# A gated linear attention and a dense gated MLP on one core: priorities of a scheduler replaced by a written order of 2439 operations

## The chip, the core and the metric

The kernel runs on one core of one Trainium2 chip. The core has five engines that each work through their own queue in order: TensorE (PE in the profile, its weight loads PEld), VectorE (DVE), ScalarE (ACT), GpSimd (POOL) and SyncE (SP), which here issues every DMA. The metric is the device time of one execution in microseconds. Three runs of the kernel before took 643.52, 644.41 and 644.46 us; the median is 644.41.

## The reference

The input has 4 batches, 8 heads, 768 time steps and 48 features per head. For each head a 48 x 48 state is carried through time. Every row of the state is multiplied by a complex decay whose size is clipped below 0.999, and the outer product of key and value is added:

```python
mag = np.sqrt(a_re * a_re + a_im * a_im)
scale = np.minimum(mag, 0.999) / (mag + 1e-06)
new_re = ar * S_re - ai * S_im
new_im = ar * S_im + ai * S_re
S_re, S_im = (new_re + k v^T, new_im)
y_t = q_t @ S_re
```

The outputs of all heads side by side are 3072 tokens of 384 features. They pass through `h = x @ w_in` (384 x 2048), `g = h * tanh(softplus(h))` and `g @ w_out` (2048 x 384). The two weight matrices arrive as 64-bit floats; everything else is float32.

## The kernel before

**Tiling.** The work is cut into 12 units (`UNITS`): three stretches of 256 time steps for each batch. A unit has two chunks, a and b, of 128 steps (`C`). A unit goes through three parts.

*Elementwise part* (`ew_steps`). From the decay come its size and its angle. Both are summed over time by scans on VectorE (lines 333 and 347). ScalarE supplies the logarithms, exponentials, arctangent and sines. The queries are multiplied by the running decay and the keys by its inverse (`grow`, line 375), and both are turned by the running angle (`rot`, line 397). The exponential and logarithm belong to one activation table, the sine and arctangent to another, so ScalarE loads a table (line 131, ACT_TABLE_LOAD) each time it passes from one to the other. The turned queries and keys are then laid out anew by DMAs from tile to tile (`relay`, line 388). Units 0 and 1 do this part chunk by chunk, the others for both chunks at once.

*Attention* (`attn_steps`). For each chunk TensorE transposes the keys (line 462), forms the 128 x 128 products of keys and queries (line 470), forms the output from them and from the old state (line 486), and the new state (line 502). VectorE masks the products (line 473) and adds the states (line 508); GpSimd fades the state (line 510), except in unit 0. The output is laid out anew by four DMAs (line 521) and split into a high part `xH` and a rest `xL` (lines 157 and 158).

*Gated MLP* (`moe_steps`). The 2048 hidden features are cut into 8 pairs of 128. For each pair `mm1` multiplies on TensorE in three terms, wH·xH, wH·xL and wL·xH (line 548, 18 matmuls), into a PSUM tile `ph`, of which there are three. ScalarE and VectorE form the gate: exp, a cap (line 553), square, ln, exp on ScalarE, a product with `ph` (line 558), then the split of the result into `gh` (line 157) and `gl` (line 158). `mm2` multiplies by the second weights, again in three terms (line 576, 12 matmuls), and adds into PSUM over the pairs. The program places `mm2` of a pair 3.5 pairs behind its `mm1`.

**Weights.** Each matrix is brought in as 12 pieces of 512 columns. The first matrix has room for all of it (`raw_in`, two halves); the second has a tile `wraw` with two buffers. `convert` turns the 64-bit pattern into a float32: ScalarE rounds the low words, VectorE shifts and joins the high ones (lines 190, 194), GpSimd adds the rounded bits (line 199), then the high part is copied on ScalarE or VectorE (line 157) and the rest subtracted on VectorE (line 158), all in one step.

**Units 0 and 1 have a halved MLP.** Their pairs are interleaved in runs of four (`slots`). With `cut`, the partial sums of the first four pairs are stored in DRAM (line 585), read back (line 588) and added (line 589), so that the second half of the weights is needed later.

**Order.** Every step gets a place on a common scale by tuned constants (`EW`, `AT`, `WP`, `LD` and others), and from it a priority. The scheduler of the language, with its own timeline model, picks the order of every engine's queue. `after` adds ordering edges, among them those that keep ScalarE's table loads together. Thirty matmuls of no use (`spin`, line 434) run on TensorE ahead of the attention and ahead of the MLP of unit 0.

## Time and profile before

| | |
|---|---|
| Three runs, median (lowest, highest) | 644.41 us (643.52, 644.46) |
| Profiled execution, span from first to last instruction | 645.8 us |
| TensorE busy (4480 matmuls) | 583.5 us, 90% |
| VectorE busy (877 instructions) | 500.8 us, 78% |
| ScalarE busy (785) | 490.7 us, 76% |
| GpSimd busy (99) | 119.9 us, 19% |
| ACT_TABLE_LOAD on ScalarE | 45 of 1283 ns |
| DMA | 67.05 MB, mean 104 GB/s |

The span is the profile's own time of the one execution it shows; the runs are timed without it. "Busy" counts the time in which an engine has an instruction at work; where two instructions of an engine overlap, that time is counted once. The granted clock (PEclk) is the share of TensorE's full clock that was granted in a stretch; matmuls take longer where it is low.

### The profile page before, as it was taken

The page shows a single profiled execution, that of the slowest core. Times are in us where ns is not written, and L with a number is a line of the kernel's source. Part 1 is how long each engine was busy: PE and PEld are TensorE (multiplying, and loading weights), DVE is VectorE, ACT ScalarE, POOL GpSimd, SP SyncE. Part 2 cuts the span into 40 slices and gives each one's busy share as a digit, 9 for nine tenths or more (in the row PEclk, how much of TensorE's full clock was granted, in tenths as well). Part 3 has the DMA queues.
Part 4 walks back from the last instruction along what each step waited for, and adds up shares of the span by engine and source line. Part 5 has one row for each costly group of instructions (what it writes and reads, how often), then busy time and mean ns, then how long its engine had stood idle before and what let it go on. Part 6 is the DMA issues. An engine that isn't in the chain of part 4 may idle for free.

```text
span 645.8 us, 11762 instructions
## 1 busy us (share of the span) xinstructions
PE 583.5 (90%) x4480; PEld 554.0 (86%) x4480; DVE 500.8 (78%) x877; ACT 490.7 (76%) x785; POOL 119.9 (19%) x99
## 2 busy tenths in 40 slices
PE   0698975888699989999999999999999999999996
PEld 0386854877699989999999999999999999999995
DVE  6989899899769869859868867977788796644551
ACT  6966977677686987977988977888898878655561
POOL 2323446326203003003003003003021030000000
PEclk9956988798899999999999999999999999999999
DMA  8859533612930450450540620711712503101000
GB/s 301 264 184 247 162 115 106 176 38 75 239 103 25 119 154 1 130 141 13 134 125 25 173 75 26 197 50 53 192 28 70 152 5 101 46 25 26 1 26 29
DMA packets 58528, 67.05 MB, mean 104 GB/s; under 512 B 4960, under 2 KB 51040, under 8 KB 58464
## 3 DMA queue, kind: packets, MB, share of 16 engines
q1 hardware_dynamic: 58464, 66.23, 35.9%
q8 instruction: 37, 0.61, 0.4%
q14 instruction: 27, 0.22, 0.1%
HBM read 36.96 MB, written 5.51 MB: 66 GB/s over the span
## 4 chain that ended last, share of the span: by engine, by line
PE 68%; DVE 12%; DMA 7%; issue 4%; POOL 3%; ACT 3%; SPq 2%; POOLq 0%; DVEq 0%
PE po L576 26%; PE ph L548 24%; PE pa L470 6%; PE ypsum L486 6%; PE pd L502 3%; DMA T<-QK 2%; PE pkn L462 2%; DVE wx L190 1%; DMA raw<-w_in 1%; POOL raw L199 1%; DMA R<-a_re 1%; DMA wraw<-w_out 1%; ACT e L123 1%; DVE e L553 1%; SPq L388 1%
## 5 line engine op out<-in xcount | busy, mean ns | idle before, releaser
L576 PE MATMUL po<-wo,gh 128*128 128x384 f32 x768 | 220.8, 348 | 11.3 <-DVE wo L157 7.4
L548 PE MATMUL ph<-xH,wiH 128*128 128x256 f32 x576 | 167.7, 293 | 6.2 <-DVE g L558 5.6
L548 PE MATMUL ph<-xL,wiH 128*128 128x256 f32 x576 | 166.9, 290 | 5.2 <-DVE xL L158 5.2
L548 PE MATMUL ph<-xH,wiL 128*128 128x256 f32 x576 | 166.6, 289 | 0.0
L123 ACT ACTIVATE e<-e 128x512 f32<-128x512 f32 x192 | 119.9, 630 | 52.8 <-DVE e L553 51.1
L576 PEld LDWEIGHTS po<-wo,gh 128*128 128x128 f32 x768 | 142.0, 190 | 16.9 <-DVE wo L157 7.7
L576 PE MATMUL po<-wo,gl 128*128 128x384 f32 x384 | 131.6, 343 | 0.0
L548 PEld LDWEIGHTS ph<-xH,wiH 128*128 128x128 f32 x576 | 112.3, 196 | 9.4 <-DVE g L558 6.0
L548 PEld LDWEIGHTS ph<-xL,wiH 128*128 128x128 f32 x576 | 113.0, 196 | 6.4 <-DVE xL L158 6.4
L548 PEld LDWEIGHTS ph<-xH,wiL 128*128 128x128 f32 x576 | 112.7, 196 | 0.0
L558 DVE SCALAR_TENSOR_TENSOR g<-e,ph 128x512 f32<-128x512 f32 x96 | 65.4, 681 | 25.5 <-ACT e L123 24.9
L553 DVE TENSOR_SCALAR e<-e 128x512 f32<-128x512 f32 x96 | 58.1, 605 | 32.9 <-ACT e L123 32.7
L123 ACT ACTIVATE e<-ph 128x512 f32<-128x512 f32 x96 | 56.8, 593 | 28.7 <-PE ph L548 28.2
L576 PEld LDWEIGHTS po<-wo,gl 128*128 128x128 f32 x384 | 73.1, 190 | 0.4 <-issue 0.4
L510 POOL TENSOR_TENSOR S<-S,T 96x384 f32<-96x384 f32 x18 | 23.0, 1279 | 266.4 <-DVE S L508 113.9
L158 DVE TENSOR_TENSOR gl<-g,gh 128x512 fp32r<-128x512 f32 x96 | 70.8, 737 | 1.6
L123 ACT ACTIVATE e<-e,fifth 128x512 f32<-128x512 f32 x96 | 69.2, 721 | 1.8
L157 DVE CAST gh<-g 128x512 fp32r<-128x512 f32 x96 | 41.4, 432 | 35.1 <-PE po L576 33.5
L375 POOL TENSOR_TENSOR QK<-QK,X 128x1536 f32<-128x1536 f32 (+1 forms) x12 | 40.2, 3353 | 103.2 <-ACT X L123 90.7
L131 ACT ACT_TABLE_LOAD x45 | 57.7, 1283 | 1.6 <-PEq L773 0.8
L470 PE MATMUL pa<-T 96*128 96x128 f32 x384 | 52.0, 287 | 0.0
L470 PEld LDWEIGHTS pa<-T 96*128 96x128 f32 x384 | 48.9, 201 | 0.9 <-issue 0.7
(88 smaller groups left out, 826.2 us busy)
## 6 DMA issues: line engine op xcount, KB each, us to landing
T<-X SPq DMA_DIRECT2D x72, 129.0 KB, 2.5
T<-QK SPq DMA_DIRECT2D x72, 129.0 KB, 3.8
raw<-w_in SPq DMA_DIRECT2D x12, 512.0 KB, 8.3
wraw<-w_out SPq DMA_DIRECT2D x12, 512.0 KB, 3.7
QK<-q SPq DMA_DIRECT2D x12, 384.0 KB, 3.9
QK<-k SPq DMA_DIRECT2D x12, 384.0 KB, 5.0
V<-v SPq DMA_DIRECT2D x12, 384.0 KB, 4.3
out_dram<-o SPq DMA_DIRECT2D x24, 192.0 KB, 1.9
```

Of the source, the lines that this page charges most:

```text
L123: ins = nc.scalar.activation(out, in_, func, **kw)
L131: ins = nc.scalar.preload_act_table_set(name)
L157: heng(h, src)
L158: leng(out=lo, in0=src, in1=h.bitcast(F32), op=ALU.subtract)
L375: (nc.vector if g in FAST and u == 0 else nc.gpsimd).tensor_tensor(QK[..., :C], QK[..., :C], X[..., :C], ALU.mult)
L470: nc.tensor.matmul(pa[:, i, :], st["T"][c][:, 4 * g + i, 1, :C], st["T"][c][:, 4 * g + i, 0, :C], start=True, stop=True)
L486: nc.tensor.matmul(py[64 * par:64 * par + D, i, :], lhs, rhs, start=n == 0, stop=first or n == 1)
L510: (nc.vector if u < WIDE else nc.gpsimd).tensor_tensor(nS, nS, pe, ALU.mult)
L548: nc.tensor.matmul(ph[:, a, :], wi[wp][:, j, kt, a * P:a * P + P], st[xp][:, kt, :], start=n == 0, stop=n == 8)
L553: nc.vector.tensor_scalar_min(e, e, math.exp(20.0))
L558: nc.vector.scalar_tensor_tensor(g, e, 2.5, ph, ALU.subtract, ALU.mult)
L576: nc.tensor.matmul(po[t], gp[:, a, tsl], wo[part][:, wp, 2 * i + a, :], start=j in starts and a == 0 and n == 0, stop=j + 1 in ends and a ...
```

## The change

All steps are recorded in a list (`Work`): for each operation its engines, a name and a function. There are 2439 of them. `ORDER` gives the sequence in which they are issued, under the language's manual schedule, so each engine's queue follows this sequence; a letter behind a number moves the operation to another of its engines. The table loads of ScalarE come wherever the written sequence passes from one table's functions to the other's.

The weights come as 16 pieces of 768 columns, one of each matrix for each pair of hidden features. A piece is loaded into one of two buffers `words` and joined into a float32 tile `w` (`weight`). Its split into high part and rest is recorded apart (`halves`); the rest is written into the tile of the piece before it.

The halved MLP with its stores and loads in DRAM is gone: all units run pairs 0 to 7. The two turns of a tile by the angle (line 397 before) are one instruction with a broadcast operand. `gl` has two buffers in place of three. Six groups of four spin matmuls stand in the order between the attention of chunk a of unit 1 and the first `mm1`. `good`, a count by which a general path is chosen when inputs are out of bounds, is kept.

```diff
-ADDV = 12
-HACT, HMOD = 2, 3
...
+WC = DM * DF // P // NPAIR
+NW = 2 * NPAIR
+SPLIT_UNITS = 2
+PLAIN = 0
+SPINS, SPIN = 6, 4
...
+ORDER = [(int(x.rstrip("VAGTS")), x.lstrip("0123456789")) for x in """
+0 1 3 6 2 4 7 127 10 340 8 560 339 30 11 5 9 13 16 343 12 27 559 132 14 17 28 19 18 31 29 20 36 32 15 21 34 33 35 24
...
+2408 2419A 2427 2398 2428 2429 2409 2420 2430 2410 2431A 2421 2432 2422 2433 2434 2435 2437 2436 2438
+""".split()]
...
+    def act(self, out, in_, func, **kw):
+        need = TABLE.get(func)
+        if need and need != self.table:
+            self.nc.scalar.preload_act_table_set(need)
+            self.table = need
+        return self.nc.scalar.activation(out, in_, func, **kw)
+
+    def issue(self, tc):
+        order = ORDER or [(i, "") for i in range(len(self.ops))]
...
+        for i, other in order:
+            engines, name, f = self.ops[i]
+            e = other or engines[0]
...
+            f(self.engines[e])
...
+    def weight(i):
...
+        def load(e):
+            words[i] = me.tile([P, WC], I64, tag="words", name="words", bufs=2)
+            e.dma_start(words[i], src)
...
+        op("S", f"w{i} load", load)
+        op("A", f"w{i} low", low)
+        op("V", f"w{i} shift", shift)
+        op("V", f"w{i} join", join)
+        op("GV", f"w{i} carry", carry)
+
+    def halves(i):
...
+        op("AV", f"w{i} high", high)
+        op("V", f"w{i} rest", rest)
...
+            op("VG", f"{n} grow", grow)
+            op("VGA", f"{n} ends q", ends("QK"))
+            op("VGA", f"{n} ends x", ends("X"))
...
+            op("V", f"{n} turn sin", turn("X", "X1"))
...
+                op("VG", f"{n} S fade", fade)
...
+                gs[j].append(me.tile([P, 2, TU], F32R, tag="gl", name="gl", bufs=2))
...
+                op("VA", f"{n} gh", high(j))
...
-    for u in range(NUN):
-        slot = slots.get(u, range(NPAIR * u, NPAIR * (u + 1)))
...
-        moe = moe_steps(units[u], u * TU, u, u < 2)
...
+    with tc.manual_schedule():
+        op.issue(tc)
...
-    with tile.TileContext(nc, schedule_with_timeline_sim=True) as tc:
+    with tile.TileContext(nc) as tc:
```

More of the change, by code (lines that the diff above doesn't have):

```diff
@@ L1 @@
 import math
-from contextlib import ExitStack
 import numpy as np
@@ L150, in tile_kernel @@
[L150 to L158 removed]
+    good = const.tile([P, UNITS + SPLIT_UNITS, 3], F32, name="good")
+    ncar = const.tile([P, NJ], F32, name="ncar")
@@ L424, in ew_steps, with load, f @@
[L424 to L437 removed]
+        def load(n, src, g):
+            def f(e):
+                x = src[u].rearrange("p (a t) -> p a t", t=C)
+                e.dma_start(flat(st[n], g), x[:, g * NJ:g * NJ + NJ] if isinstance(g, int) else x)
+            return f
@@ new lines, in load_qk, with f, load_v @@
+        def load_qk(a, src):
+            def f(e):
+                e.dma_start(both(st["QK"], slice(0, NCH))[:, :, a, :C], src[u].rearrange("p (a t) -> p a t", t=C))
+            return f
+        def load_v(e):
+            st["V"] = io.tile([P, NCH, DM], F32, tag="V", name="V", bufs=2)
+            e.dma_start(st["V"], v[u])
+        agroups = groups if u == 0 else (slice(0, NCH),)
+        for g in agroups:
+            op("S", f"R{u} load {gi(g) if u == 0 else u}", load("R", are, g))
+            op("S", f"I{u} load {gi(g) if u == 0 else u}", load("I", aim, g))
@@ L494, in yv @@
-                return f
-            def upd():
-                nS = at.tile([2 * D, H, D], F32, tag="S", name="S", bufs=2)
-                for g in range(2):
-                    pd = bank([2 * D, 4, D], "pd", "pd", c)
+                                lhs = st["V"][:, c, h * D:(h + 1) * D] if new else old["S"][:, h, :]
+                                rhs = d["am", h // 4][:, h % 4, :] if new else T()[:, h, 0, :C]
+                                e.matmul(ypsum[64 * par:64 * par + D, i, :], lhs, rhs,
+                                         start=m == 0, stop=first or m == 1)
@@ new lines, in f, with fade @@
+                        e.tensor_tensor(d["S"][:, sl, :], d["pd", g], old["S"][:, sl, :], ALU.add)
+                return f
+            def fade(e):
+                pe = T()[:, :, 0, C].unsqueeze(2).broadcast_to([2 * D, H, D])
+                e.tensor_tensor(d["S"], d["S"], pe, ALU.mult)
+            if not last:
+                for g in range(2):
+                    op("T", f"{n} kn{g}", kn(g))
+                    op("AV", f"{n} kn out{g}", kn_out(g))
+            for g in range(2):
+                op("T", f"{n} am{g}", am(g))
+                op("V", f"{n} am out{g}", am_out(g))
@@ new lines, in chunk, with move, f @@
+            for g in range(2):
+                op("T", f"{n} y{g}", y(g))
+            op("AV", f"{n} y out", y_out)
+            if not last:
+                for g in range(2):
+                    op("T", f"{n} pd{g}", pd(g))
+                    op("V", f"{n} S add{g}", add(g))
+                op("VG", f"{n} S fade", fade)
+        for c in range(NCH):
+            chunk(c)
+        def move(p0, j, r0, n):
+            def f(e):
+                e.dma_start(st["x"][p0:p0 + 4 * n, j, :], st["y"][r0:r0 + n].rearrange("r i t -> r (i t)"))
+            return f
@@ new lines, in attention, with high, f, rest @@
+        for r, run in enumerate(XRUNS):
+            op("S", f"u{u} x move{r}", move(*run))
+        if u < PLAIN:
+            return
+        def high(j):
+            def f(e):
+                (e.copy if e is nc.scalar else e.tensor_copy)(st["xH"][:, j], st["x"][:, j])
+            return f
+        def rest(j):
+            def f(e):
+                e.tensor_tensor(st["xL"][:, j], st["x"][:, j], st["xH"][:, j].bitcast(F32), ALU.subtract)
+            return f
+        for j in range(NJ):
+            op("AV", f"u{u} xH{j}", high(j))
+            op("V", f"u{u} xL{j}", rest(j))
```

892 lines of the change are left out of this document (415 added, 477 removed), and 16 rows, old and new, of the table ORDER.

## Prediction

> **What bounds the kernel now.** I read the page first, for the shares of the engines; then busy time in windows, to find where TensorE is not full; then the chain of waits, for the price of TensorE's work; then the groups of instructions of two stages.
>
> ```profile
> span 645.8 us, 11762 instructions
> PE 583.5 (90%) x4480; PEld 554.0 (86%) x4480; DVE 500.8 (78%) x877; ACT 490.7 (76%) x785; POOL 119.9 (19%) x99
> ```
>
> ```profile
> 0.00:16.00 16.00, 0.00 (x0) 0.00 (x0) 10.77 (x28) 11.01 (x20) 4.35 (x18) 1.00 0.86 301
> 16.00:160.00 144.00, 113.15 (x744) 97.89 (x746) 135.23 (x233) 109.84 (x184) 61.52 (x40) 0.81 0.51 152
> 160.00:240.00 80.00, 72.41 (x560) 70.29 (x556) 62.25 (x113) 61.39 (x99) 9.96 (x7) 0.96 0.49 133
> 240.00:384.00 144.00, 143.11 (x1170) 137.58 (x1167) 115.55 (x197) 120.66 (x188) 18.37 (x14) 1.00 0.33 92
> 384.00:416.00 32.00, 32.00 (x263) 31.68 (x262) 28.34 (x47) 26.89 (x44) 6.43 (x5) 1.00 0.32 89
> 416.00:639.60 223.60, 222.88 (x1757) 216.58 (x1756) 148.67 (x266) 160.40 (x255) 19.30 (x15) 1.00 0.22 59
> 639.60:646.00 6.40, 0.00 (x0) 0.00 (x0) 0.00 (x0) 0.49 (x1) 0.00 (x0) 0.82 0.21 69
> ```
>
> The columns are the stretch, its length, the busy time of PE, PEld, DVE, ACT and POOL, the granted clock, and DMA. There are three stages. **Stage 1**, to 160 us: VectorE is busy 10.77 + 135.23 = 146.0 us, from 16 us on 94% of the time, while TensorE waits and runs at a clock of 0.81. **Stage 2**, 160 to 384 us: TensorE is almost full; VectorE has 62.25 + 115.55 = 177.8 us of 224 and ScalarE 61.39 + 120.66 = 182.05. **Stage 3**, to 639.6 us: TensorE is full. The last matmul ends there, and 6.2 us of output follow.
>
> TensorE's work at full clock has these prices:
>
> ```profile
> 173.48 1.51 PE pkn L462 x8
> ...
> 259.21 2.12 PE po L576 x12
> 261.33 2.12 PE ph L548 x18
> 263.45 1.90 PE ypsum L486 x32
> ...
> 269.79 1.32 PE pd L502 x16
> ...
> 284.77 1.78 PE pa L470 x16
> ...
> 635.48 4.10 PE po L576 x22
> ```
>
> Twelve units have 96 pairs at 2.12 + 2.12 us, 20 chunks at 1.51 and at 1.32, 24 at 1.78 and 22 at 1.90 (four chunks have no old state): 407.0 + 56.6 + 84.5 = 548 us. The last matmul ends at 639.6 us, so 91.5 us are lost before it. After 160 us there were 479.6 us, of which 9.2 were idle by the windows and 4% of 72.4 lost to the clock: 467.5 us of work. So 548 − 467.5 = 80.5 us are done by 160, the loss is 79.5 us in stage 1, 11.7 in stage 2 (224 us for 212.3 of work) and under 1 in stage 3.
>
> **The change part by part.** The matmuls are the same. I count the written order off from its end with the prices above. 467.5 us of TensorE's work are left behind the `mm1` of pair 4 of unit 1 (166 half `mm1` and 176 half `mm2` at 1.06 us, and 132 attention groups), and 253 behind the first `mm1` of pair 2 of unit 6. These two places end stages 1 and 2 of the new kernel. Then I count what VectorE, ScalarE and GpSimd have ahead of each.
>
> *VectorE in stage 1, work moved.* I price what differs from the trace, in which 22 of 24 weight pieces and 11 pairs were through by 160 us.
>
> ```profile
> L158 DVE TENSOR_TENSOR wiL<-raw,wiH 128x512 fp32r<-128x512 f32 x12 | 9.6, 800 | 1.7 <-ACT wiH L157 1.7
> ...
> L375 DVE TENSOR_TENSOR QK<-QK,X 128x768 f32<-128x768 f32 x2 | 1.9, 946 | 0.1
> ```
>
> Five of 16 carries move from GpSimd to VectorE. The nearest row is the subtraction, 0.80 us for 512 columns, so 1.2 for 768: +6.0 us (0.64 a carry if it ran at the 0.43 us that a one-operand instruction takes below: +3.2). The `grow` of units 1 and 2 moves too, four such halves at 0.946: +3.8. All weights instead of 22 of 24 are ready, about +4.7; three more fades, small copies, +2. Against that only one high part of 16 is copied on VectorE, before seven of 24, −3; three `gh` go to ScalarE and fewer pairs are begun, −4; the turns, squares and angles of this stretch are fewer, −4.5. The sum is about +5.
>
> *VectorE in stage 1, stalls.* One and the same instruction, the cap at line 553, is long while GpSimd works and short otherwise:
>
> ```profile
> 301.36 2.10 DVE L553 TENSOR_SCALAR e<-e 128x512 f32<-128x512 f32 x1
> ...
> 306.68 0.43 DVE L553 TENSOR_SCALAR e<-e 128x512 f32<-128x512 f32 x1 [0.18 <-ACT e L123]
> ```
>
> ```profile
> 299.58 3.59 POOL L375 TENSOR_TENSOR QK<-QK,X 128x1536 f32<-128x1536 f32 x1 [25.76 <-ACT X L123]
> ```
>
> The long one ends 0.3 us behind the end of GpSimd's `grow`. The groups of stage 1 carry the same excess, the first and second here:
>
> ```profile
> L190 DVE TENSOR_SCALAR wx<-raw 128x512 uint32<-128x512 uint32 x12 | 11.5, 955 | 0.0
> ...
> L355 DVE COPY ncar<-I 128x3 f32<-128x3 f32 x3 | 2.6, 863 | 0.0
> ```
>
> ```profile
> L199 POOL TENSOR_TENSOR raw<-raw 128x512 int32<-128x512 int32 x12 | 19.8, 1659 | 29.2 <-DVE raw L194 28.0 <-ACT wiH L157 1.1
> ```
>
> Line 190 at 0.955 instead of 0.43 is 6.3 us too long, and with the other groups, each against the shortest of its shape, I count 20.8 us. GpSimd was busy 4.35 + 61.52 = 65.9 us in this stage. In the written order it has 11 carries and nothing else up to the stage's end: 11 x 1.659 x 1.5 = 27 us. If the excess falls with GpSimd's time, 12 us of the 20.8 go; bounds 0 and 20.8. So VectorE needs 146.0 + 5 − 12 = **139 us** (130 to 155).
>
> The Trainium skill (SBUF — State Buffer, Who interferes with whom) says that VectorE and GpSimd lock a port for a whole instruction and that whichever comes second waits it out; the two rows agree. By it 11 carries can still hold up VectorE 11 times for up to 2.5 us, 27 us, so that all of the excess could stay: stage 1 would then be 12 us longer than I say below.
>
> *ScalarE.* Counted along the order, it changes its table 17 times in stage 1 (13 in the trace), 30 in stage 2 (18), 61 in all (45).
>
> ```profile
> L131 ACT ACT_TABLE_LOAD x13 | 16.7, 1283 | 1.0 <-PEq L773 0.8
> ```
>
> ```profile
> L131 ACT ACT_TABLE_LOAD x18 | 23.1, 1283 | 0.3
> L123 ACT ACTIVATE X<-X 128x768 f32<-128x768 f32 x15 | 12.7, 848 | 0.0
> ```
>
> ```profile
> L157 ACT CAST wiH<-raw x8: 635/664/690, 27.3 to 127.7; 128x512 fp32r<-128x512 f32 x8
> ```
>
> ```profile
> 309.21 1.28 ACT L131 ACT_TABLE_LOAD   x1
> 310.51 0.85 ACT L143 ACTIVATE X<-I 128x768 f32<-128x768 f32 x1
> ```
>
> Stage 1: 4 loads are 5.1 us, high copies of 15 pieces at 1.0 instead of 15 at 0.66 another 5, and `gh`, small copies and the earlier start of the next units some 5: 120.85 + 15 = 136 us, still below VectorE's. Stage 2: 12 loads are 15.4 us; 75 elementwise operations of 768 columns stand in it for 60, 15 x 0.85 = 12.8; 7 `gh` at 0.66 are 4.6; fewer copies out of PSUM and no weights, −5. That is +28, and since ScalarE's groups of this stage add up to 196.8 us for 182.05 busy (neighbours overlap), +26: **208 us** of ScalarE against 212.3 of TensorE. VectorE, by the same count, comes to some 195. Stage 3 is left with under 190 us for each of them against 253.
>
> The Trainium skill (ScalarE: Activation LUTs, What ACT_TABLE_LOAD costs) adds a drain of about 1.38 us to each switch. The two rows above show the next operation 0.02 us behind the load, so I leave it out; by the page, an estimate, 30 switches would put 41 us more on ScalarE in stage 2.
>
> *How long the stages are then.* The unknown is how full an engine that bounds can be kept. VectorE as the bound of stage 1 was 94% busy (135.23 of 144), with single windows at both ends:
>
> ```profile
> 32.00:48.00 16.00, 15.98 (x105) 14.26 (x103) 13.01 (x28) 9.88 (x19) 4.49 (x6) 0.50 0.56 193
> ...
> 96.00:112.00 16.00, 9.03 (x52) 8.50 (x51) 16.00 (x18) 11.12 (x15) 10.75 (x7) 0.82 0.37 107
> ```
>
> ```profile
> 352.00:416.00 64.00, 63.98 (x531) 61.92 (x530) 52.75 (x90) 55.34 (x86) 7.33 (x6) 1.00 0.39 107
> ```
>
> I take 94% for both bounds. Stage 1: 16 + (139 − 10.8)/0.94 = **152 us**, 8 less. Stage 2: 208/0.94 = **221 us**, 3 less than 224. Stage 3 and the output stay. So the span is 645.8 − 11 = 635; the runs' median is 1.4 below the profiled span, which gives **634 us**.
>
> *Edits that I cost at nothing.* Dropping the halves saves four stores, four loads and four additions on VectorE, which the counts above hold already or are coarser than. The spins are 24 for 30 and run while TensorE has nothing else; none stands ahead of unit 0's attention now, which at clock 0.50 takes twice its 12 us, hidden since TensorE has 79.5 us to lose in stage 1; without that cover, 12 us. Two `gl` buffers make VectorE wait for the `mm2` two pairs back, with the caps and gates behind it; in the order that `mm2` always stands ahead of the `gl`, by at least two operations, and such a wait can only grow where TensorE is late, that is, full. The tail of the order ends with ten half `mm2`, as the trace ends with a run of such matmuls.
>
> **Weights through two buffers.** The first matrix had room for itself; now 16 pieces share two buffers.
>
> ```profile
> raw<-w_in SPq DMA_DIRECT2D x12, 512.0 KB, 8.3
> wraw<-w_out SPq DMA_DIRECT2D x12, 512.0 KB, 3.7
> ```
>
> A piece has 768 KB: 5.6 us by the lower row, 12.5 by the upper, and about 5 until its carry frees the buffer (1.0 + 1.0 + 2.5 and gaps). That is 5.3 to 8.8 us a piece and 85 to 140 us for all. The last piece is wanted by pair 7 of unit 0, where VectorE has 95% of its stage 1 work behind it, at 144 us. I take the lower row, since the upper is from six loads issued at once, and it is hidden.
>
> **The rivals.**
>
> *ScalarE becomes the bound of stage 2 and is served worse (slower).* Its queue is in order; square, ln and exp of a pair wait for VectorE's cap, and all that stands behind waits too. For it: 208 against 212.3 us leaves no slack, and ScalarE was never above 86% (55.34 of 64) over any long window while TensorE was full. Against: nothing asked it for more. At 86.5% stage 2 takes 240 us: +16 − 8, span 654, median **653**. It decides from 208/(224 + 8) = 90% downward.
>
> *Both bounds are kept full (much faster).* All waits of stage 1 behind 16 us go, and stage 2 is TensorE's 212.3: 16 + 128 = 144 and 212, −16 − 12, median **617**. For it: windows of 16.00 us of 16. Against: three engines above 92% at once, which no stage of the trace shows.
>
> *The weights come late (no change).* With 12.5 us a load and some queueing behind relays on SyncE's queue, pair 7 of unit 0 slips by 8 us and the gain of stage 1 is gone; with ScalarE below 94%, 3 us of stage 2 too: **644**.
>
> *The order isn't what decides (the change doesn't do what it says).* If a table switch did cost a second 1.3 us, stage 2 would be 247/0.94 = 263 us and the median 673; the gap of 0.02 us speaks against it.
>
> **How the numbers follow.** Forecast, both bounds near 94%, median 624 to 643: 0.54. Both full: 0.14. ScalarE served worse: 0.21. Late weights: 0.10, over half of it within 0.2%. A costlier switch: 0.01. Faster by over 0.2%, about what a measurement of this kernel can tell from no change, is then 0.54 + 0.14 + 0.02 = 0.70; the same 0.07; slower 0.23. The range for 8 in 10 goes from both full, 617, to ScalarE served worse, 653. The likeliest case's own range is 624 to 643.
>
> **What would show it.**
>
> ```profile
> L553 DVE TENSOR_SCALAR e<-e 128x512 f32<-128x512 f32 x96 | 58.1, 605 | 32.9 <-ACT e L123 32.7
> ```
>
> Right: TensorE's share passes 95% before 155 us, VectorE busy over 94% ahead of that, ScalarE at 90% or more from then to about 370 us, 61 table loads, caps near 0.5 us in the mean instead of 0.605. Wrong: TensorE idle in stage 2 waiting for the gate, with VectorE in turn waiting for ScalarE (the first rival); the shift of a piece waiting for its DMA beyond 100 us (late weights); or VectorE's stalls unchanged in spite of 27 us of GpSimd. The forecast falls if VectorE's work up to pair 4 of unit 1 comes out above 150 us.

## The result and the profile after

The changed kernel takes **652.72 us** (median of 16 runs, 649.04 to 655.73), the kernel before 645.0 us beside it (16 runs, 641.98 to 652.46). The ratio is 1.0121, with an interval of 1.0098 to 1.0143: slower by some 8 us, where 634 was forecast. The profiled execution of after is the slowest of its 16 (655.73 us, span 653.9), 3 us above their median; profiles of two kernels below, whose time is not told apart from after's (`gh` on VectorE, four `g`), were taken at 651 us, and where the 3 us matter I use these too.

The head of the page of after:

```profile
span 653.9 us, 11597 instructions
PE 577.9 (88%) x4474; PEld 551.5 (84%) x4474; DVE 489.5 (75%) x853; ACT 510.6 (78%) x808; POOL 60.5 (9%) x37
```

VectorE has 11 us less to do than before, ScalarE 20 us more, GpSimd half. TensorE's work is the same. I cut the span of after at the prediction's own places, where 467.5 and 253 us of TensorE's work are left; they fall at 162 and 389 us (forecast: 152 and 373; in the profile with `gh` on VectorE, at 651 us, 158 and 381). Busy time in windows, columns as in the prediction (length, PE, PEld, DVE, ACT, POOL, clock, DMA):

```profile
0.00:16.00 16.00, 0.00 (x0) 0.00 (x0) 9.11 (x21) 13.48 (x23) 2.29 (x15) 1.00 0.86 287
16.00:162.00 146.00, 105.31 (x751) 95.29 (x752) 133.78 (x217) 118.94 (x191) 23.26 (x11) 0.85 0.53 160
162.00:240.00 78.00, 77.05 (x620) 75.19 (x619) 70.39 (x123) 73.39 (x113) 5.66 (x2) 1.00 0.36 99
240.00:389.00 149.00, 140.75 (x1116) 135.01 (x1116) 122.75 (x208) 130.65 (x201) 18.10 (x5) 0.98 0.37 103
389.00:647.00 258.00, 254.43 (x1992) 245.93 (x1991) 153.43 (x287) 173.27 (x283) 11.15 (x5) 1.00 0.20 54
```

The amounts of work came out nearly as costed. VectorE has 9.11 + 133.78 = 142.9 us ahead of 162 us (139 forecast), ScalarE 73.39 + 130.65 = 204 us in stage 2 (208). What did not come is the time: in this profile stage 1 ends 10 us later than forecast, stage 2 lasts 227 us and not 221, and the rest 3 us longer.

Where the 8 us lie is seen by laying the stretches of the trace of before over the one of after. First after, in the windows that the prediction shows of before:

```profile
16.00:160.00 144.00, 103.31 (x737) 93.29 (x738) 131.78 (x213) 116.99 (x188) 23.26 (x11) 0.85 0.53 161
160.00:240.00 80.00, 79.05 (x635) 77.19 (x634) 72.39 (x127) 75.34 (x117) 5.66 (x2) 1.00 0.36 100
240.00:384.00 144.00, 135.75 (x1081) 130.05 (x1081) 118.78 (x200) 125.67 (x192) 18.10 (x5) 0.98 0.36 103
384.00:480.00 96.00, 92.42 (x733) 88.45 (x732) 71.70 (x132) 81.96 (x130) 6.80 (x3) 1.00 0.34 91
```

and the one window of before that was not shown:

```profile
384.00:480.00 96.00, 95.32 (x776) 92.72 (x775) 78.03 (x135) 80.73 (x127) 12.21 (x10) 1.00 0.34 92
```

From 160 to 240 us TensorE is busy 79.05 us, before 72.41: the change gains 6.6 us there. From 240 to 480 it is busy 135.75 + 92.42 = 228.2 us, before 143.11 + 95.32 = 238.4: 10 us lost again. The same from the records of the matmuls: I price those that start behind a given time as the prediction does; the time up to the last matmul less that work is what TensorE loses behind it. In us:

| TensorE's loss | up to 144 us | 144 to 240 | behind 240 | all |
|---|---|---|---|---|
| before | 73.4 | 16.0 | 1.6 | 91.0 |
| after (profile at 655.7) | 81.1 | 0.2 | 17.6 | 98.9 |
| after with `gh` on VectorE (651.3) | 77.1 | 0.3 | 17.3 | 94.7 |
| after with four `g` (651.6) | 77 | 0.8 | 17.1 | 95 |

So the change wins 16 us between 144 and 240 us, pays 16 behind 240, and some 4 to 8 ahead of 144. The first column differs by 4 us between the last three rows, which have the same order; differences of that size in it are not evidence alone.

The traces of after and of `gh` on VectorE part at one transfer. The load of piece 6 (the pieces are counted from 0) is issued at 52.9 and 52.6 us; it lands after 7.2 us in after and after 4.6 in the other, and VectorE's shift of this piece waits for it, first in after:

```profile
60.13 0.56 DVE L256 TENSOR_SCALAR w<-words 128x768 uint32<-128x768 uint32 x1 [2.99 <-DMA words<-w_in]
```

```profile
57.21 1.04 DVE L256 TENSOR_SCALAR w<-words 128x768 uint32<-128x768 uint32 x1 [1.07 <-DMA words<-w_in]
```

The shift of piece 5 stands 1.0 us later in after, that of piece 6 2.9 us, and every one behind it 2.3 to 3.1 us: one load that lands late goes with a whole stage that comes late. Why it landed late these traces do not show.

In the groups of after, table loads, caps, `gh`, and the carries on GpSimd and on VectorE (count | busy, mean ns | idle before):

```profile
L164 ACT ACT_TABLE_LOAD x61 | 78.3, 1283 | 1.0
L668 DVE TENSOR_SCALAR e<-e 128x512 f32<-128x512 f32 x96 | 44.5, 465 | 32.4 <-ACT e L166 32.0
L627 ACT CAST gh<-g 128x512 fp32r<-128x512 f32 x37 | 22.7, 615 | 7.7 <-DVE g L621 7.1 <-DVE e L668 0.5
L264 POOL TENSOR_TENSOR w<-w,words 128x768 int32<-128x768 int32 x11 | 23.6, 2149 | 117.7 <-DVE w L260 73.2 <-ACT words L166 13.5 <-ACT e L166 12.2
L264 DVE CUSTOM_DVE_ANT_0 w<-words,w 128x1536 uint16<-128x1536 uint16 x5 | 4.7, 944 | 0.0
```

The prediction's signs hold here: 61 loads with 1.0 us of idle time ahead of all of them, caps at 0.465 us in place of 0.605.

From the waits of after between 16 and 160 us (engine, what waits, for what: us in total, times, longest), TensorE's three longest and VectorE's for the pieces:

```profile
PE pkn L497 <- DMA T<-QK: 29.8, 2, 28.2
PE pkn L497 <- DMA R<-a_re: 11.1, 1, 11.1
PE ph L609 <- DVE g L621: 8.1, 2, 6.4
...
DVE w L256 <- DMA words<-w_in: 4.1, 2, 3.0
...
DVE w L256 <- DMA words<-w_out: 2.3, 3, 1.1
```

and some of those between 160 and 480 us:

```profile
DVE QK L429 <- DMA T<-QK: 8.7, 3, 3.4
ACT X L166 <- DMA R<-a_re: 5.3, 1, 5.3
DVE gl L633 <- ACT gh L627: 4.1, 1, 4.1
DVE QK L423 <- DMA QK<-q: 4.1, 1, 4.1
PE ph L609 <- DVE g L621: 7.0, 8, 2.1
```

TensorE's longest wait is the one for its first transposes, which start at 28.2 us; in before they start at 28.2 us too. Then it waits 11.1 us once from 72.7 us on, and 6.4 us from 106.6 us on for a gate. The work that it has done (priced as above) is 23.7 us at 88 us, where before has 37.8, and 48.4 at 128 us, where before has 56.5. Behind 240 us the waits are single ones of 3 to 5 us for transfers, at the head of VectorE's and ScalarE's queues, and TensorE waits for the gate behind them.

### The profile page after: what moved, and what is told of

Its sections match the earlier page's. It is cut to its first block, busy times and chain, and to the rows that moved or that the text cites. A ratio compares the mean times of both kernels' runs of the same rounds, so it can differ in the third digit from the quotient of the medians.

```text
span 653.9 us, 11597 instructions
## 1 busy us (share of the span) xinstructions
PE 577.9 (88%) x4474; PEld 551.5 (84%) x4474; DVE 489.5 (75%) x853; ACT 510.6 (78%) x808; POOL 60.5 (9%) x37
## 5 line engine op out<-in xcount | busy, mean ns | idle before, releaser
L609 PE MATMUL ph<-xH,wh 128*128 128x256 f32 x504 | 148.1, 294 | 14.3 <-DVE g L621 14.2
L609 PE MATMUL ph<-xL,wh 128*128 128x256 f32 x504 | 143.5, 285 | 0.5 <-DVE xL L592 0.5
L609 PE MATMUL ph<-xH,wl 128*128 128x256 f32 x504 | 143.4, 284 | 0.0
L166 ACT ACTIVATE e<-e 128x512 f32<-128x512 f32 x192 | 117.2, 626 | 17.3 <-DVE e L668 16.3
L644 PE MATMUL po<-wh,gh 128*128 128x384 f32 x336 | 118.7, 353 | 3.7 <-ACT gh L627 3.7
L644 PE MATMUL po<-wh,gl 128*128 128x384 f32 x336 | 116.2, 346 | 0.8 <-DVE gl L633 0.6
L644 PE MATMUL po<-wl,gh 128*128 128x384 f32 x336 | 115.6, 344 | 0.0
L609 PEld LDWEIGHTS ph<-xH,wh 128*128 128x128 f32 x504 | 97.0, 192 | 19.3 <-DVE g L621 15.7
L609 PEld LDWEIGHTS ph<-xL,wh 128*128 128x128 f32 x504 | 96.9, 192 | 0.8 <-DVE xL L592 0.8
L609 PEld LDWEIGHTS ph<-xH,wl 128*128 128x128 f32 x504 | 96.9, 192 | 0.0
L164 ACT ACT_TABLE_LOAD x61 | 78.3, 1283 | 1.0
L644 PEld LDWEIGHTS po<-wh,gl 128*128 128x128 f32 x336 | 64.7, 193 | 1.7 <-DVE gl L633 1.5
## 6 DMA issues: line engine op xcount, KB each, us to landing
T<-X SPq DMA_DIRECT2D x72, 129.0 KB, 2.5
T<-QK SPq DMA_DIRECT2D x72, 129.0 KB, 2.5
```

Source lines behind the costliest of these rows:

```text
L164: self.nc.scalar.preload_act_table_set(need)
L166: return self.nc.scalar.activation(out, in_, func, **kw)
L609: e.matmul(ph[j][:, a, :], win(x, j, kt, a), st[y][:, kt, :], start=n == 0, stop=n + 1 == len(todo))
L644: e.matmul(po[t], x[:, a, t * P:(t + 1) * P], wout(y, j, a), start=j == 0 and a == 0 and n == 0, stop=j + 1 == NPAIR and a == 1 and n + 1 ...
```

## The experiments

The kernel before was run beside each, on the same chip; its medians lay between 643.7 and 645.9 us, and each ratio is to it. An edit's gain is stated against after's 652.7; a ratio whose interval overlaps 1.0098 to 1.0143 is not told apart from after's.

### Does VectorE bound stage 1?

**gh_on_vectore.** All 37 `gh` that the order gives to ScalarE go back to VectorE.

```diff
-741 174 569 ... 246 212 247A 439 575 ...
+741 174 569 ... 246 212 247 439 575 ...
```

> All 37 copies gh that the written order puts on ScalarE go back to VectorE; nothing else changes. ScalarE gets 37 x 0.615 = 22.8 us less, VectorE 37 x 0.42 = 15.5 us more. Theory S (ScalarE is too full in stage 2: 208 us of work and 61 table loads): the 17.6 us that TensorE loses after 160 us shrink by about a third or more, 5 to 8 us faster, 645 to 648 us. Theory T (operations that wait for transfers stand at the heads of VectorE's and ScalarE's queues, with the gates behind them): the waits for T, QK, x and R stay where they are, no change within 2 us, 651 to 655.

Measured 653.37 us, ratio 1.0133 (1.0088 to 1.0178).

**no_join.** VectorE's join of the weights' high words is left out; that part of the computation is missing.

```diff
         def join(e):
-            e.scalar_tensor_tensor(x, word(1), 0xC0000000, x, ALU.bitwise_and, ALU.bitwise_or)
+            return
```

> The join of each of the 16 pieces (sign and exponent bits put to the shifted word) is left out, so the weights, and with them the output, are not those of the reference; order, transfers and all else stay. VectorE gets 16 x 0.945 = 15.1 us less, all of it in stage 1, nearly three times what leaving out the caps took from it there. Theory V (VectorE's work sets the end of stage 1): 12 to 16 us faster, 637 to 641 us. Theory W (transfers, relays and TensorE's clock set it as much): 3 to 7 us, 646 to 650 us, and VectorE's idle time of stage 1 grows by the rest.

Measured 650.78 us, ratio 1.0093 (1.0065 to 1.0121), not told apart from after. The window of stage 1, first of gh_on_vectore, then of no_join:

```profile
16.00:160.00 144.00, 105.69 (x763) 95.28 (x764) 136.76 (x223) 119.15 (x190) 22.62 (x11) 0.88 0.53 163
```

```profile
16.00:160.00 144.00, 105.83 (x762) 96.19 (x763) 125.96 (x206) 120.21 (x193) 22.98 (x11) 0.89 0.52 160
```

This is the pair that decides. VectorE has 136.76 us of work in the one and 125.96 in the other, 11 us apart, and TensorE did 105.69 and 105.83. A whole instruction less on each of 16 pieces, 16 x 0.95 = 15 us, brought 2 us. By the records of the matmuls TensorE has done 82.8 us of work by 160 us in gh_on_vectore and 82.6 in no_join, so even these 2 us do not lie in stage 1. **VectorE's work does not set the length of stage 1.** By the prediction's formula no_join would have had 15/0.94 = 16 us.

**four_g.** The gate's tile `g` has four buffers in place of three.

```diff
-                g_[j] = me.tile([P, 2, TU], F32, tag="g", name="g", bufs=3)
+                g_[j] = me.tile([P, 2, TU], F32, tag="g", name="g", bufs=4)
```

> Four buffers instead of three for g (which the output tile o shares); nothing else. Theory T (waits at the heads of in-order queues after stage 1): a gate that follows the two output tiles of a unit waits for a store to land (1.5 us at 400 us in the trace); with the fourth buffer these waits go, 1 to 3 us faster. If the buffers of the pairs play no part: no change within 1 us.

Measured 654.17 us, ratio 1.0151 (1.0086 to 1.0216). A fourth buffer brings nothing that shows.

### Does ScalarE bound stage 2?

**no_table_loads.** Arctan and sine are replaced by squares, so that one table serves; that part of the computation is another.

```diff
+        func = {AF.Arctan: AF.Square, AF.Sin: AF.Square}.get(func, func)
         need = TABLE.get(func)
```

> Arctan and the two sines are replaced by Square, so that ScalarE loads one table at the start and never changes it; the output is no longer that of the reference, order and all other operations stay. ScalarE gets 60 x 1.28 = 77 us less, 38 of them in stage 2 where the change had added 15. Theory S: most of the 17.6 us after 160 us go, 10 to 15 us faster, 638 to 643. Theory T: only what ScalarE itself had queued behind goes, 0 to 4 us, 649 to 653, and the waits of VectorE for T<-QK and QK<-q stay.

Measured 648.74 us, ratio 1.0059 (1.0032 to 1.0086), told apart from after. Sixty loads of 1283 ns, 77 us of ScalarE's time, are gone, and 4 us come back. Its window and waits behind 160 us:

```profile
240.00:480.00 240.00, 229.57 (x1835) 221.44 (x1834) 189.03 (x336) 169.08 (x289) 26.41 (x9) 0.99 0.36 99
```

```profile
DVE QK L430 <- DMA T<-QK: 8.2, 3, 3.4
ACT X L167 <- DMA R<-a_re: 5.7, 1, 5.7
DVE QK L424 <- DMA QK<-q: 4.7, 1, 4.7
PE ph L610 <- DVE g L622: 8.5, 5, 2.9
```

ScalarE is at 169.08 of 240 us, 70%, and TensorE is busy 229.57, after 228.17. The waits are after's, of the same size. Its loss behind 240 us is 15.6 us by the records. So a ScalarE that is too full is not the reason either. The loads themselves cost their 1283 ns and no more: ScalarE's busy time falls from 510.6 to 433.2 us, 77.4 for 60 loads. The Trainium skill (ScalarE: Activation LUTs, What ACT_TABLE_LOAD costs) adds a drain of about 1.38 us to a switch; with it 60 loads would have taken 160 us of ScalarE's time, an estimate by that figure, and neither the 1.0 us of idle time ahead of 61 loads nor these 77.4 us show it.

**no_cap.** The cap of `e`, VectorE's step amid ScalarE's chain of a pair, does nothing.

```diff
-            op("V", f"{n} cap", lambda e, j=j: e.tensor_scalar_min(e_[j], e_[j], math.exp(20.0)))
+            op("V", f"{n} cap", lambda e: None)
```

> The cap of every pair is left out (with these inputs it changes no value), so VectorE gets 96 x 0.47 = 45 us less, 12 x 0.51 = 6.2 us of it in stage 1, and square no longer waits for VectorE. If VectorE's work sets the end of stage 1 (as the prediction had it), stage 1 ends 6 to 7 us earlier. After stage 1, theory S: nothing more than 2 us, since ScalarE has as much to do as before. Theory T: VectorE is blocked as long as before, nothing more than 2 us either. A gain of 10 us or more in all would say that it is the chain from engine to engine of each pair, not one engine's load or one transfer, that costs.

Measured 649.05 us, ratio 1.0054 (1.0027 to 1.008), told apart from after. The loss behind 240 us falls from 17.6 to 13.1 us. With 96 instructions of 0.465 us gone, 45 us of VectorE's time, 3.7 us come back. Here a step is out of the chain that a pair passes through ScalarE and VectorE, and in no_table_loads the loads are out of ScalarE's queue, in which such steps stand.

### The weights

**half_pieces.** From piece 2 on only half of the columns are loaded, into the buffer of two pieces ahead; the rest are old words, so the result is another.

```diff
-            words[i] = me.tile([P, WC], I64, tag="words", name="words", bufs=2)
-            e.dma_start(words[i], src)
+            words[i] = words[i - 2] if i > 1 else me.tile([P, WC], I64, tag="words", name="words", bufs=2)
+            n = WC if i < 2 else WC // 2
+            e.dma_start(words[i][:, :n], src[:, :n])
```

> From the third piece on, a load of a weight piece brings 384 KB instead of 768 KB (the other half of the buffer keeps the words of an earlier piece, so the output is no longer the reference's); every operation on the pieces stays as it is. Theory W (the pieces' transfers hold up stage 1: VectorE waits 6.4 us for words, and the relays of chunk b of unit 1, which stand behind two pieces on the same transfer queue, land 6.6 us after their issue, while TensorE is idle for 11.1 us): stage 1 ends 4 to 7 us earlier, total 645 to 648 us. Theory V (VectorE's 143 us of work set the end of stage 1): those waits are only exchanged for others, no change within 2 us.

Measured 648.39 us, ratio 1.0048 (1.0017 to 1.0078): 4.3 us, as much as any edit gained. In its window VectorE and TensorE both do more than in after (131.78 and 103.31), since all of the stage comes earlier:

```profile
16.00:160.00 144.00, 109.52 (x787) 99.84 (x787) 141.04 (x225) 124.12 (x199) 24.06 (x11) 0.88 0.43 123
```

Its loss up to 144 us is 73.5. What the bytes hold up is seen on SyncE's queue of after (start, length, what is issued), with the relays of `X` and `QK` among two pieces:

```profile
71.49 1.27 SPq L454 DMA_DIRECT2D T<-X  x2
72.86 0.54 SPq L249 DMA_DIRECT2D words<-w_out  x1
73.45 0.56 SPq L454 DMA_DIRECT2D T<-X  x1
74.36 0.33 SPq L249 DMA_DIRECT2D words<-w_in  x1
75.69 2.19 SPq L454 DMA_DIRECT2D T<-QK  x3
77.94 0.61 SPq L336 DMA_DIRECT2D R<-a_re  x1
```

and by the landing times of tile `T` in this window, first of after, then of half_pieces:

```profile
DMA to landing us min/median/max: 6.2/6.2/6.6
```

```profile
DMA to landing us min/median/max: 3.2/3.7/4.0
```

A relay of 129 KB takes 2.5 us in the median of the run (page, `T<-QK SPq DMA_DIRECT2D x72, 129.0 KB, 2.5`). Behind two pieces of 768 KB it takes 6.2, behind two half pieces 3.7. The matmuls `pkn` (the transposes of the keys) of unit 1's second chunk wait for these relays: the last of them lands at 83.5 us, and `pkn` starts at 83.8. The view names the load of `R`, but that lands at 84.3 us, behind the start.

**relays_first.** Is that wait, 11.1 us at 72 us, what stage 1 loses? The relays go ahead of the two pieces, and 51 operations around them are moved to suit (names in place of numbers).

```diff
-w7 high, w9 load, u1a S add1 ... w10 load, u1b turn cos ... u1b relay cos0, R3 load 3
+w7 high, u1a S add1 ... u1b turn cos, w2 rest ... u1b relay cos0, w9 load, w10 load, R3 load 3
```

> 54 neighbouring operations of stage 1 are put in another order, the rest stands as written: the loads of pieces 9 and 10 go behind the cosine relays of chunk b of unit 1 instead of ahead of them, the steps on these two pieces behind the last subtraction of piece 2, and the first layer of pair 1 of unit 0 ahead of that chunk's transposes. TensorE's wait of 11.1 us at 72 us gets shorter by the 3 us or so by which the relays land earlier, and pair 1 runs in it; but pieces 9 and 10, and with them all later ones, come some 4 us later. Theory W (the relays behind the pieces, and TensorE idle for them, set the end of stage 1): 3 to 6 us faster, 646 to 650 us. Theory P (the chain of the pieces through their two buffers sets it: load, ScalarE, VectorE, carry, next load): 2 to 5 us slower, 654 to 658 us, although TensorE waits less there.

Measured 653.64 us, ratio 1.0126 (1.0086 to 1.0165): nothing. Ahead of the pieces the three relays of `QK` landed after 2.3 to 2.5 us, at 77.2 and not at 83.5 us. The one wait became three of 4.3, 3.8 and 2.2 us, and the piece behind (11) was loaded at 83.9 us as against 83.3. Neither expectation's number came. The wait was there, but the time was not its.

**carry_on_vectore.** The 11 carries of GpSimd go to VectorE, so that GpSimd rests in stage 1.

```diff
-368 128 129 25 37 44 130 26 131 45 ...
+368 128 129 25 37 44 130 26 131V 45 ...
```

> The 11 carries that the written order gives to GpSimd go to VectorE. VectorE gets 11 x 0.94 = 10.4 us more in stage 1; GpSimd has nothing to do there any more, so the 13.8 us by which VectorE's instructions of stage 1 are longer than the shortest of their shape should go if GpSimd is what makes them long: VectorE's busy time changes by about -3 us. Theory V: stage 1 ends 3 us earlier. If the excess stays at 10 us or more, GpSimd is not its cause, VectorE has 8 us more to do, and under theory V the total gets 8 us worse; under theory W (pieces' transfers) it moves by less than 3 us either way.

Measured 650.44 us, ratio 1.0085 (1.0047 to 1.0123); 2.3 us, not told apart. But it shows what a carry costs its neighbours. The scans of the angle ahead of 162 us, first in after, then here, and the carries here:

```profile
L406 DVE TENSOR_TENSOR_SCAN X<-rmask,I 128x384 f32<-128x384 uint8 x8 | 12.6, 1570 | 0.1
```

```profile
L407 DVE TENSOR_TENSOR_SCAN X<-rmask,I 128x384 f32<-128x384 uint8 x8 | 7.6, 948 | 0.1
L265 DVE CUSTOM_DVE_ANT_0 w<-words,w 128x1536 uint16<-128x1536 uint16 x16 | 15.2, 950 | 0.0
```

With every VectorE instruction up to 162 us held against the short end of its shape (the tenth percentile), the excess is 23.4 us in before, 13.8 in after and 1.5 here. The 11 carries lengthened VectorE by 12.3 us, 1.1 each. On VectorE they cost 11 x 0.95 = 10.4 us. The Trainium skill (SBUF — State Buffer, Who interferes with whom) says that VectorE and GpSimd lock a port pair against each other; the trace agrees, with 1.1 us for a carry of 2.15.

**before_carry.** In the kernel before, the carries go to VectorE too, with the joined word in `wx`.

```diff
-        nc.vector.scalar_tensor_tensor(hi, hi, 0xC0000000, x, ALU.bitwise_and, ALU.bitwise_or)
+        nc.vector.scalar_tensor_tensor(x, hi, 0xC0000000, x, ALU.bitwise_and, ALU.bitwise_or)
...
-            nc.gpsimd.tensor_tensor(hi, hi, lo, ALU.add)
+            nc.vector.tensor_tensor(hi, hi, lo, ALU.add)
```

> The kernel before, with its 24 carries of 512 columns on VectorE and not on GpSimd; the halved MoE and the language's scheduler stay. VectorE gets 24 x 0.63 = 15 us more; if GpSimd's carries are what lengthens VectorE's instructions there too, some 18 of the 23.4 us of excess in stage 1 go (40.4 of GpSimd's 65.9 us), so VectorE's stage 1 gets 0 to 3 us shorter. Theory V (VectorE's work sets the end of stage 1): 0 to 3 us faster, 642 to 645. If the excess lay in time that VectorE had to spare: up to 10 us slower.

Measured 662.49 us, ratio 1.029 (1.0238 to 1.0342). The window of stage 1:

```profile
16.00:160.00 144.00, 108.43 (x703) 93.65 (x704) 123.38 (x225) 97.93 (x168) 27.92 (x18) 0.76 0.51 149
```

VectorE was *less* busy than in before (123.38 us for 135.23): by the code of this edit the one buffer of `wx` stays occupied until the split, and the next piece must wait for it. The 17 us lie outside both expectations. The run mixes two things and decides nothing on before.

**no_spin.** The 24 spins are left out.

```diff
-        junk = ps.tile([P, 512], F32, tag="po", name="junk", bufs=2)
+        return
```

> The 24 spins, which run from 52 to 61 us, are left out; the order stays. If they hold TensorE's clock up for unit 0's first pairs and unit 1's attention: clock below 0.6 from 64 to 96 us, and up to 3 us slower. If they only use up what the clock allows (0.61 from 64 to 80 us, right behind them): clock above 0.8 there, and up to 4 us faster. If TensorE has time to spare there, as the prediction had it: no change within 1.5 us.

Measured 656.65 us, ratio 1.0171 (1.0141 to 1.02): 3.9 us slower by the medians, with intervals that just touch: by the rule above not told apart from after, if barely. The windows where the spins stood, and the next, of no_spin:

```profile
48.00:64.00 16.00, 7.48 (x43) 6.80 (x44) 12.80 (x18) 8.04 (x14) 6.71 (x3) 0.59 0.70 226
64.00:112.00 48.00, 27.20 (x221) 25.21 (x220) 43.31 (x65) 39.03 (x61) 6.51 (x3) 0.75 0.53 158
```

and of after:

```profile
48.00:64.00 16.00, 13.42 (x74) 8.79 (x75) 11.96 (x17) 8.60 (x16) 6.64 (x3) 0.79 0.75 231
64.00:112.00 48.00, 28.22 (x215) 25.74 (x213) 43.85 (x65) 38.60 (x60) 6.62 (x4) 0.71 0.53 158
```

The granted clock from 48 to 64 us falls from 0.79 to 0.59 without them. That the 3.9 us come from this is not shown. From 64 to 112 us the clock is higher without the spins (0.75 for 0.71), and from 64 to 96 it is 0.67, not below 0.6 as the first expectation had it. TensorE then waits for the same relays in both, 13.8 us without the spins and 11.1 with them, and has done the same work: 20.7 us at 80 us in both, and 63.1 (no_spin) and 62.9 (after) at 144 us. The loss up to 144 us is 80.9 us here and 81.1 in after's profile, in both behind a late piece 6 (VectorE waits 2.8 and 3.0 us for it).

### Is it the order?

**own_scheduler.** The same operations with the written order as priorities only; the language's scheduler queues them, as in before.

```diff
-    with tc.manual_schedule():
-        op.issue(tc)
+    op.issue(tc)
...
+            tc.cur_priority = 1000 * (k + 1)
...
-    with tile.TileContext(nc) as tc:
+    with tile.TileContext(nc, schedule_with_timeline_sim=True) as tc:
```

> The same 2400 operations on the same engines, with the written order given only as a priority: the language's scheduler orders every queue by its own cost model, as it does in the kernel before; the table loads are tied to their operations. If the operations (61 table loads, 37 gh on ScalarE, 16 pieces, one QK buffer) are what costs, the time stays at 648 to 657 us. If the fixed order is what costs (theory O), the time comes down towards the kernel before or below it, 635 to 645.

Measured 689.56 us, ratio 1.0668 (1.0608 to 1.0728). Its page:

```profile
span 689.2 us, 11611 instructions
PE 590.8 (86%) x4474; PEld 554.2 (80%) x4474; DVE 498.9 (72%) x853; ACT 514.7 (75%) x807; POOL 58.9 (9%) x37
```

VectorE and ScalarE are as busy as in after within 2% (498.9 and 514.7 us), and the run takes 37 us longer (loss 90.2, 9.6 and 34.9 us in the table's three stretches). To these operations the written order is worth 37 us against this scheduler; operations and order together still lose 8 us to before. Neither expectation came.

**order_late, order_early, order_all; order_near, order_near_tables.** Can another order do better? I planned the sequence anew from the durations in the traces: behind 150 us, ahead of it, and all of it (with `order_late` leaving the first 548 places as they are); then two planned with more terms, the first kept near the written one (1.3 to 1.8 places moved in the mean on TensorE's, ScalarE's and VectorE's queues), the second less near with fewer table loads.

```diff
-(order_late)  ... 330 754 625 626 331 623 483 ...
+(order_late)  ... 330 626 623 331 473 625 332 ...
-(order_early) 0 1 3 6 2 4 7 127 10 340 ...
+(order_early) 0 1 3 2 6 127 7 340 10 339 ...
-(order_near)  0 1 3 6 2 4 7 ...
+(order_near)  0 7 1 3 6 2 4 ...
```

> Only the order is changed, and only behind the 150 us mark: the operations that start before it stand as written; the rest are ordered anew on all engines, by durations read from the traces of the changed kernel, so that an operation that would wait for a transfer or another engine stands behind what is ready (table loads fall from 61 to 35). Operations, engines, tiles and buffers are the same. Theory T (after stage 1, TensorE's loss of 17.6 us comes from waits at the heads of in-order queues): most of the 17.6 us go, 10 to 15 us faster than the changed kernel, 637 to 643 us. If the loss is in the operations themselves or in the buffers: no change within 3 us, 649 to 655.

> The other half: operations up to the 150 us mark are ordered anew, those behind it stand as written. Theory W or any theory by which stage 1 is set by when the transfers, the relays and the pairs of unit 0 stand in the queues: stage 1 ends 5 to 9 us earlier, 643 to 648 us, with VectorE's work unchanged at about 143 us. Theory V (VectorE's work sets the end of stage 1, at 92 to 94% busy): there is at most 3 us to be had.

> The order is made anew from the first operation to the last (27 table loads); operations, engines, tiles and buffers are those of the changed kernel. If the order alone makes up both losses, they add: 628 to 636 us, faster than the kernel before by 1.5% or more. If the operations or VectorE's work set the time: 645 us or more.

> The order of the changed kernel with small moves alone: 1576 of the operations change their place in their engine's queue, on VectorE by 1.8 places in the mean, on TensorE by 1.3; table loads fall from 61 to 53. The moves were chosen with durations that count what the last three runs had shown and the orders before left out: 0.035 us from one engine to the next, the time a last matmul takes to come out, VectorE's stalls behind GpSimd, transfers one after another. Theory M (operations and work are right; an order loses what its durations leave out): 8 to 15 us faster than the changed kernel, 638 to 645 us, with the loss after 160 us under 10 us. Theory N (no order of these operations gets below the changed kernel by much, since VectorE and ScalarE are too full): 648 us or more.

> As the run before it, but with the operations that need the second table gathered, 29 table loads instead of 61, which takes 41 us from ScalarE at the price of moves of 4.5 places on ScalarE and 6.6 on VectorE in the mean. Theory M with the table loads mattering as little as in the run without any (4 us for all of them): within 3 us of the run before it, 638 to 645 us. If larger moves bring back what the re-made orders lost: 650 us or more.

| | us | ratio (interval) | loss to 144 / to 240 / behind |
|---|---|---|---|
| order_late | 661.05 | 1.0219 (1.0185 to 1.0253) | 79.9 / 11.1 / 17.1 |
| order_early | 665.11 | 1.0305 (1.0278 to 1.0332) | 89.1 / 2.0 / 17.4 |
| order_all | 672.06 | 1.0432 (1.0372 to 1.0493) | 89.2 / 9.0 / 14.9 |
| order_near | 660.3 | 1.0248 (1.0192 to 1.0303) | 85.8 / 3.7 / 13.7 |
| order_near_tables | 665.89 | 1.0311 (1.0246 to 1.0377) | 86.6 / 8.2 / 13.9 |

All are 8 to 19 us slower than after. order_late loses 11 us between 144 and 240, where after loses 0.2, and the four that differ ahead of 144 lose 5 to 8 us more there than after's 81.1. Only the last column became smaller, by up to 4 us. A plan from the durations of a trace does not hit what the chip does to a microsecond, and in fixed queues each miss can become a wait; that this is the reason is likely and not shown. The stretch behind 160 us of order_late, which was full in after:

```profile
160.00:240.00 80.00, 74.59 (x533) 72.13 (x532) 68.67 (x120) 66.90 (x105) 5.06 (x2) 0.94 0.36 99
```

**near_late, near_late_carry.** The order of order_near from the 619th place on only, with after's ahead of it; the second also with all carries on VectorE.

```diff
-... 509 769 492 520 502 493 510 ...
+... 509 492 635 636 502 503 520 ...
```

> The order as written up to the 170 us mark, and behind it the order of the run with small moves, whose loss from 240 us on was 13.7 us for 17.6 while its first 130 us had gone 5 us worse. Theory M: stage 1 as in the changed kernel, and 4 us or more less loss behind it, 645 to 649 us. Theory N (what is moved out of one wait comes back in another): no change within 2 us, 651 to 655, or worse.

> As the run before it, and the 11 carries of GpSimd on VectorE, which alone had brought 2.3 us. If stage 1 and what follows it add up: the run before it less 2 us. If the earlier end of stage 1 only moves the operations against an order that was made for other times: the same as the run before it within 1 us.

Measured 650.22 us (1.0107, 1.0061 to 1.0153) and 650.56 us (1.0087, 1.0061 to 1.0112). The loss behind 240 us falls from 17.6 to 11.3 and 10.8, about 6.5 us, and 2 of them are lost again ahead of 240; by the runs' times 2.5 and 2.2 us are gained, not told apart from after. The carries add nothing to the moved order. None of the 18 kernels beats before.

## Why the prediction was wrong, by its own steps

**The step that failed** is the first line of "How long the stages are then": stage 1 as 16 + (139 − 10.8)/0.94 = 152 us. The sizes in it were right within a few us; that VectorE's work decides was not. VectorE's excess fell by 23.4 − 13.8 = 9.6 us (12 forecast), its work by 162 us was 142.9 (139), its fill (busy share) 133.78/146 = 92% (94%). Put into the formula, these sizes give after's 162 us, some 6 us of the miss from the work behind 16 us and 4 from the fill; but that only describes the stage, for the formula fails when the work is changed: no_join and gh_on_vectore, 11 us of VectorE's work apart, had TensorE at 105.8 and 105.7 us. A busy share of 94% said that VectorE is nearly always at work, and not that the stage gets shorter when it has less.

**What stands in its place.** In after the stage moves as a block: the earlier the last piece is done, the more work TensorE has done by 160 us, one us for one. In the 12 profiles with after's order up to 160 us (but for relays_first's 51 moves), TensorE's work done by 160 us and the time at which the last piece's subtraction ends add up to 225.1 to 226.0: after 78.8 and 146.5, no_join 82.7 and 142.4, half_pieces 86.4 and 139.2. And from the subtraction of piece 3 to the shift of piece 14 it took 26.0 us in after, 26.0 in no_join, 25.8 to 26.6 in nine of these profiles, and 24.7 and 24.6 in no_cap and no_table_loads. VectorE is busy 25.3 of the 26.0 us in after and 23.4 of 26.0 in no_join: taking the joins from it only lengthened its waits between these points. What did move the block: the bytes of the pieces (4.3 us by the runs; the last subtraction ends at 139.2 us, in the others between 141.1 and 146.5), the steps of a pair's chain through ScalarE and VectorE (1.4 us in this stretch), and, from one profile to the next without any edit to the weights, by the two traces above, the landing of piece 6 (some 3 us). That the stage is a chain of hand-overs between fixed queues is what these runs agree with; a single one that sets it was looked for in relays_first and not found, so which of them does stays open. The last piece's load stood at 131.0 us behind 12 relays and a load of `R`, though its buffer was free from 117.3 us; this was seen and not tried.

**Stage 2** as 208/0.94 = 221 us failed in the same way. ScalarE had 204 us in 227, 90%, and with 77 us less of it 4 us came back. TensorE was full from 144 to 240 us, better than forecast, and lost 17.6 us later. Of that, 4.5 went with the caps and some 6.5 with small moves of the order. The 2 that went with the table loads are no evidence: no_join, whose edit ends with the last piece near 142 us, has some 15 in this column as well. Waits for transfers of `T`, `QK` and `R` stayed in their places with ScalarE at 70%; that they are the rest is likely from the waits and not shown, and no run took them away.

**Stage 3** as unchanged: 264.9 us from 389 us to the end, against 261.8 us; 3 of the 17.6 us lie in it (TensorE 254.43 of 258).

**The rivals.** *ScalarE served worse* gave 653 us, the measured time to half a microsecond, and its sign was seen (TensorE waits for the gate, ScalarE at 90%, the point it named). Its mechanism was not: it took stage 1 as 8 us shorter and ScalarE as the engine that decides stage 2; the first did not come, and no_table_loads speaks against the second. The range of 617 to 653 us holds the measured time only at the edge that this rival gave it. A right time is no proof of a mechanism. *Late weights* was partly so: the shift waits for its DMA 6.4 us in all, 3.0 of them once at piece 6, and half the bytes are worth 4.3 us; but the shifts' waits lie ahead of 100 us and not at the end, where that rival put them. *Both full* needed what no stage showed. *A costlier switch* is out: 61 loads, 1.0 us of idle time ahead of them.

**Costed at nothing.** Spins: 3.9 us by the medians, where the prediction saw them as filling TensorE's empty time; the clock beside them is lower without them, but where the 3.9 us lie stays open. The weights through two buffers: 4.3 us by the bytes, where 5.6 us a piece was held to be hidden. `gl` waits 4.1 us once, and the wait is put down to `gh`, not to the `mm2` that frees its buffer; it ends at 299.0 us, 3.5 us behind ScalarE's wait of 5.3 us for `R`. gh_on_vectore, where `gh` is VectorE's own, is no faster. The halved MLP was not tried alone, so what dropping it cost is open.

**What was right:** 61 loads without a drain, caps at 0.465 us, GpSimd's 23.6 us (27 forecast), the fall of VectorE's excess with GpSimd's time, and TensorE full before 155 us: its window from 128 us on, of after,

```profile
128.00:144.00 16.00, 15.80 (x125) 15.11 (x126) 13.41 (x22) 10.35 (x16) 4.40 (x2) 0.89 0.32 107
144.00:160.00 16.00, 16.00 (x144) 15.56 (x143) 15.00 (x30) 14.64 (x24) 0.00 (x0) 1.00 0.32 100
```

The prediction took this as the end of stage 1. But the 467.5 us of work that it counted behind this point were left at 162 us and not at 152: TensorE was fed later ahead of 128 us (48.4 us of work done there, 56.5 in before).

## What to carry to other kernels

An engine that is 94% busy while another waits is not by that the bound: where several in-order queues hand work to each other, test it by taking work away before dividing work by a fill. A written order fixes each engine's queue for one set of durations; it can be worth 37 us to its operations and still not pay for slower feeding, and plans made from the durations of a trace lost 8 to 19 us on the chip. Count also what a transfer makes late behind it. And hold an edit against more than one trace of the same order: two of them differ by 4 us here, most of it from one load on.

## What the runs showed of the hardware

- GpSimd's carry of 2.15 us lengthened VectorE by 1.1 us (12.3 us for 11), most plainly in the scans: 1570 ns in place of 948.
- With 24 matmuls of no use the granted clock was 0.79 over 16 us, without them 0.59; over the 48 us behind it was 0.71 and 0.75. The kernel was 3.9 us shorter with them by the medians, and the profiles do not show it in this stage.
- A 129-KB relay behind two 768-KB pieces landed after 6.2 us, behind two half pieces after 3.7, ahead of the pieces after 2.3 to 2.5, in the run's median after 2.5. One 768-KB load of the same order landed after 7.2 us in one run and after 4.6 in another.
- A table load cost ScalarE 1283 ns and nothing ahead of it that shows (1.0 us for 61); without 60 of them the kernel was 4 us shorter, not 77.
